# The first chunk's sums over the taps move from VectorE to TensorE, and the low products go to the end of their sums

## The chip, the cores and the metric

The kernel runs on one core of one Trainium2 chip. The metric is the device time of one execution in microseconds; the median of three runs of the kernel before is 1714.68 us (1714.65 to 1714.75).

## The reference

Two steps, all in float32. First a light convolution: for each of 33280 positions (8 sequences of 4160) and each of 8 heads, seven weights are made by a softmax, and the output is the weighted sum of the last seven rows of `x` (192 channels, 24 to a head). Then a feed-forward layer with a maximum over three products.

```python
w = np.exp(weight_gen - max over the 7 taps); w = w / (w.sum(-1) + 1e-09)
x_unf = x_pad[:, idx, :]                  # the 7 rows that end at each position
out = np.einsum('bshk,bskhg->bshg', w, x_unf)          # (33280, 192)
h = np.maximum(np.maximum(out @ w1, out @ w2), out @ w3)   # 192 -> 768
return h @ w_out                                        # 768 -> 192
```

The weights of the feed-forward layer arrive as float64.

## The kernel before

The 33280 positions lie as 128 partitions of 260 rows each. A chunk is 4 rows per partition, 512 positions; there are 65 chunks. The first chunk is a "super" of its own, after it three chunks share one load of `x` (tile xt) and of the tap weights (wt).

For a chunk the work goes like this. GpSimd multiplies `x` with the tap weights, one of the four rows at a time, into r (128 partitions, 192 channels by 7 taps; three buffers; L246, `product`). VectorE sums r over the taps into acc (L261, `total`). The sum is turned round: for the first three chunks by TensorE, with `nc.tensor.transpose` against the identity into two PSUM banks (L276 for channels 0 to 127, L277 for the other 64; `transpose`), for later chunks by VectorE and ScalarE. Then it is split into a high and a low float32r part, so that products of rounded parts give a float32 result: xa_hi and xa_lo for the first 128 channels, xb and xc for the rest (`parts`: L300 and L306, L308 on ScalarE, L304 and L309 on VectorE for the first three chunks).

The feed-forward weights are split likewise, and this happens once, in the opening. A piece goes through these steps in `split`: ScalarE's absolute value (L467) into a PSUM bank, three VectorE operations (L469, L471, L476), ScalarE's copy into the high part (L481), three more on VectorE that overwrite the bank or fill e (L483, L488, L492), ScalarE's f (L494), and GpSimd's product f times e into the low part (L495). The pieces have names in the program: a0 to a8 are the first 128 channels (wa_hi, wa_lo; 256 columns each), b0 to b2 the other 64 (wb_hi, wb_lo; 384 columns each, with four extra ScalarE copies, L550), d0 to d5 the last matrix (wo).

TensorE's main loop has for each chunk nine steps `up`, each two sums of 512 columns: per sum products wa_hi with xa_hi, wa_hi with xa_lo, wa_lo with xa_hi, wb_hi with xb, and in part wb_lo with xc (all at L329). The 128 rows are worked as two halves of 64 that run side by side. ScalarE copies the first of three sums to m (L376), VectorE takes the maximum with the other two (L378), ScalarE and GpSimd split the result into h_hi and h_lo (L381, L385). Four `down` tasks then multiply the chunk before with wo. The PSUM pool "ph" has eight banks, for transposes, weight pieces and sums alike.

The order of all that stands around TensorE's loop is written by hand. Time is counted in ticks, 22 to a chunk. `OPENING` maps a tick to a list of stages: `a0` carries piece a0 one step on, `s0` a softmax, `x0.1` is the product of chunk 0, row 1, `+0.1` its sum, `t0` one row's turn, `p0` a step of the split. Tick -1 holds what comes before the loop. A stage whose forerunner isn't done does that first (`stage` calls `finish`). What `OPENING` doesn't name goes by the rule tables: `ticks` places `+c.t` at 22 times (c minus a chunk count) plus a tick, from `SUMS`. Every engine keeps the order in which the instructions were written (`pin`).

Of the kernel before, what the change touches and what calls it, by code (L numbers as in the profile page):

```python
# [20 lines left out]
P = 128  # L21
# [3 lines left out]

OPENING = {
    -1: (
        "x0.0 s0 x0.1 a0 s0 a0 a0 x0.2 a0 a2 t0 +0.0 a2 b0 +0.1 a1 b0 b0 a1 +0.3 s1 a3 b0 a1 "
        "a2 s1 a1 +0.2 t0 b1 s1 x0.3"
    ),  # L30
    0: "a6 a4 a2 a3 a6",
    1: "a6 a3 b0 t0 t0",
    2: "b1 a6 s0",
    3: "a4 a5 a3",
    4: "b1 a5",
    6: "b2 +1.0 a5 x1.1 x1.0",
    7: "x1.2 s1 a4",
    8: "+1.1",
    9: "a5 b2 x1.3",
    10: "b2 b2 b1 p0",  # L40
    11: "s0 t1 +1.2",
    12: "a4 +1.3",
    14: "b1 p0",
    16: "a7 a7 a8 p1",
    17: "a7 t1",
    18: "s2 d1 d1 a8 p1",
    19: "p1 b2 a8 d2 t1",
    20: "d2 p0 d1",
    21: "d0",
    22: "d0",  # L50
    24: "a7 +2.0 d0",
    25: "d2 +2.1 d1",
    26: "d3 t1",
    27: "d0 x2.1 d3 d5 d2",
    28: "d3 x2.2",
    29: "x2.3 d3 a8 d4",
    30: "d4 x2.0",
    31: "d5",
    32: "+2.2 d4 d5",
    33: "t2 +2.3 t2 t2",  # L60
    34: "s2",
    35: "x3.0 x3.2 p2",
    36: "d4",
    38: "d5 p2 p2",
    42: "x3.1",
    43: "t3 t3",
    46: "+3.3 +3.2 +3.1 +3.0 t2",
    48: "t3",
    49: "s2",
    52: "x4.1",  # L70
    54: "t3",
    56: "x4.0 p3",
    57: "x3.3",
    58: "p3 t3 s2",
    59: "t3",
    61: "+4.1",
    66: "x4.2",
    67: "x4.3",
    68: "t3",
    69: "p3",  # L80
    74: "+4.3 +4.2",
    77: "+4.0",
}


# [7 lines left out]
LOAD = (5, 5)  # L93

ON_TENSOR = 3


@with_exitstack
def lightconv_maxout_kernel(
# [25 lines left out]
    nc = tc.nc  # L125
    B, S, D = x.shape
    H, K = weight_gen.shape[2:]
# [48 lines left out]
    state = {}  # L176

    def pin(ins):

        tc.keep_in_program_order(ins)  # L180
        return ins
# [52 lines left out]
    def product(c, t):  # L234

        s = super_of[c]
        a, n = chunks[c]
        la = a - chunks[supers[s][0]][0]
        xt, wt = state["x", s], state["w", s]
        if t == 0:  # L240
            state["acc", c] = att.tile([P, TC, D], F32, name="acc")

        r = att.tile([P, D, K], F32, name="r", bufs=3)
        state["r", c, t] = r
        pin(
            nc.gpsimd.tensor_tensor(  # L246
                r.rearrange("p (h g) k -> p k h g", g=G),
                xt[:, la + t : la + t + K].rearrange("p k (h g) -> p k h g", g=G),
                wt[:, la + t]
                .rearrange("p (h k) -> p k h", k=K)  # L250
                .unsqueeze(3)
                .broadcast_to([P, K, H, G]),
                op=ALU.mult,
            )
        )

    def total(c, t):

        r = state.pop(("r", c, t))
        pin(  # L260
            nc.vector.tensor_reduce(  # L261
                state["acc", c][:, t], r, axis=AX.X, op=ALU.add
            )
        )

    def transpose(c):


        acc = state["acc", c]
        if c < ON_TENSOR:  # L270
            pa, pb = (ps.tile([P, CH], F32, name="ph") for _ in range(2))
            pb = pb[:DB]
            state["p", c] = pa, pb
            for t in range(TC):
                to = slice(t * P, (t + 1) * P)
                pin(nc.tensor.transpose(pa[:, to], acc[:, t, :P], ident))  # L276
                pin(nc.tensor.transpose(pb[:, to], acc[:, t, P:], ident))  # L277
                yield
            return
        v = xtp.tile([P, NJ * D * 2], F32, name="room", bufs=1)  # L280
        pa, pb = v[:, :CH], v[DB:, CH : 2 * CH]
        state["p", c] = pa, pb
        blocks = v[:, 2 * CH : 2 * CH + TC * D].rearrange("p (t d) -> p t d", t=TC)
        pin(nc.vector.transpose(blocks, acc))  # L284
        yield
        for f in range(0, D, 32):
            to = pa[f : f + 32] if f < P else pb[f - P : f - P + 32]
            to = to.rearrange("f (t p) -> f t p", t=TC)
            for p in range(0, P, 32):
                pin(nc.scalar.copy(to[:, :, p : p + 32], blocks[p : p + 32, :, f : f + 32]))  # L290
            yield

    def parts(c):
# [8 lines left out]

        eng, at = (nc.vector, halves[0]) if c < ON_TENSOR else (nc.gpsimd, halves[1])
        pin(eng.tensor_tensor(xa_lo, pa, xa_hi.bitcast(F32), op=ALU.subtract))  # L304
# [20 lines left out]
    def product_of(ph, terms, half, key, begins=True, ends=True):  # L325

        h = halves[half]
        for q, (n, w, v) in enumerate(terms):
            ins = nc.tensor.matmul(  # L329
                ph[:, :n],  # L330
                w[h],
                v[h],
                start=begins and half == 0 and q == 0,
                stop=ends and half == 1 and q == len(terms) - 1,
            )
# [242 lines left out]
    def stage(name):  # L578
# [19 lines left out]
    def finish(name):  # L598
        while stage(name) != "done":
            pass  # L600
# [32 lines left out]
    for c in range(NC + 1):  # L633
        for tick in range(TICKS):
# [10 lines left out]
            k, odd = divmod(tick - (TC if tick >= 2 * DOWN_AT else 0), 2)  # L645
# [5 lines left out]
            if c == NC:  # L651
# [4 lines left out]
                elif tick >= 2 * DOWN_AT + TC and tick < 2 * DOWN_AT + 2 * TC:  # L656
                    t = tick - 2 * DOWN_AT - TC
# [44 lines left out]
```

## Time and profile before

| | |
|---|---|
| median of three runs | 1714.68 us |
| the profiled execution | 1714.73 us |
| its span, first to last instruction | 1712.9 us |
| TensorE busy, matmuls | 1668.9 us, 97% |
| GpSimd busy | 1427.9 us, 83% |
| ScalarE busy | 1138.6 us, 66% |
| VectorE busy | 1135.5 us, 66% |
| L261, the sums over the taps | 260 of them, 401.9 us, mean 1547 ns |
| L276 and L277, transposes on TensorE | 12 of each |

Rows of a timeline show the start in microseconds, the length, the engine, the line, the operation with output and inputs, and in brackets how long the engine stood idle before and what ended that. Lengths of neighbours on one engine overlap a little, so the distance from start to start is what an instruction costs in a queue. The chain rows show a start, a length and whose work it is. The view by stretches gives for each engine the busy microseconds and the instructions in that stretch.

### The profile page before, as it was taken

The page shows a single profiled execution, that of the slowest core. Times are in us where ns is not written, and L with a number is a line of the kernel's source. Part 1 is how long each engine was busy: PE and PEld are TensorE (multiplying, and loading weights), DVE is VectorE, ACT ScalarE, POOL GpSimd, SP SyncE. Part 2 cuts the span into 40 slices and gives each one's busy share as a digit, 9 for nine tenths or more (in the row PEclk, how much of TensorE's full clock was granted, in tenths as well). Part 3 has the DMA queues.
Part 4 walks back from the last instruction along what each step waited for, and adds up shares of the span by engine and source line. Part 5 has one row for each costly group of instructions (what it writes and reads, how often), then busy time and mean ns, then how long its engine had stood idle before and what let it go on. Part 6 is the DMA issues. An engine that isn't in the chain of part 4 may idle for free.

```text
span 1712.9 us, 42123 instructions
## 1 busy us (share of the span) xinstructions
PE 1668.9 (97%) x16794; PEld 1639.7 (96%) x16794; DVE 1135.5 (66%) x1570; ACT 1138.6 (66%) x2878; POOL 1427.9 (83%) x844
## 2 busy tenths in 40 slices
PE   3799999999999999999999999999999999999999
PEld 2589999999999999999999999999999999999999
DVE  7967666666666666766666666666666666666653
ACT  3556667667667667666766766766766766676672
POOL 5888888989888888888888898988889888888872
PEclk9999999999999999999999999999999999999999
DMA  7010101101010110101010110101011010101000
GB/s 234 1 69 11 69 20 60 69 20 60 20 70 10 70 43 38 69 20 67 13 70 20 60 69 20 60 20 69 11 69 49 31 69 20 69 11 46 20 11 29
DMA packets 20422, 79.50 MB, mean 46 GB/s; under 512 B 2321, under 2 KB 5129, under 8 KB 17537
## 3 DMA queue, kind: packets, MB, share of 16 engines
q1 hardware_dynamic: 20104, 76.54, 11.8%
q8 instruction: 131, 2.15, 0.5%
q14 instruction: 67, 0.54, 0.1%
q10 hardware_dynamic: 120, 0.28, 0.1%
HBM read 51.25 MB, written 25.56 MB: 45 GB/s over the span
## 4 chain that ended last, share of the span: by engine, by line
PE 94%; DVE 4%; DMA 1%; issue 0%; SPq 0%; ACT 0%; DVEq 0%; ACTq 0%
PE ph L329 94%; DVE acc L261 1%; DVE m L378 1%; DVE ph L471 0%; DVE e L492 0%; DVE ph L476 0%; DMA h_lo<-in_moe_w_dram 0%; DVE ph L488 0%; DVE ph L469 0%; DVE ph L483 0%; DMA xt<-in_x_dram 0%; SPq L526 0%; DVE red L215 0%; SPq L518 0%; DVE xb L309 0%
## 5 line engine op out<-in xcount | busy, mean ns | idle before, releaser
L246 POOL TENSOR_TENSOR r<-xt,wt 128x1344 f32<-128x1344 f32 x260 | 721.8, 2817 | 0.7 <-DMA xt<-in_x_dram 0.4
L378 DVE TENSOR_TENSOR m<-ph,m 128x512 f32<-128x512 f32 x780 | 522.8, 685 | 215.4 <-PE ph L329 115.8
L385 POOL TENSOR_TENSOR h_lo<-m,h_hi 128x512 fp32r<-128x512 f32 x390 | 503.3, 1302 | 169.3 <-ACT h_hi L381 164.5
L329 PE MATMUL ph<-xa_hi,wa_hi 64*128 64x512 f32 x2340 | 627.5, 390 | 5.6 <-ACT f L494 3.4
L329 PE MATMUL ph<-xa_lo,wa_hi 64*128 64x512 f32 x2340 | 624.8, 388 | 2.5 <-DVE xa_lo L304 2.5
L329 PE MATMUL ph<-xa_hi,wa_lo 64*128 64x512 f32 x2340 | 624.3, 388 | 2.8 <-POOL wa_lo L495 2.7
L329 PE MATMUL ph<-xb,wb_hi 64*128 64x512 f32 x2340 | 623.9, 387 | 0.0
L329 PE MATMUL ph<-wo,h_hi 64*128 64x384 f32 x3120 | 596.1, 358 | 0.0
L329 PE MATMUL ph<-wo,h_lo 64*128 64x192 f32 x3120 | 554.9, 249 | 0.0
L381 ACT CAST h_hi<-m 128x512 fp32r<-128x512 f32 x390 | 242.0, 621 | 403.9 <-DVE m L378 400.9
L329 PEld LDWEIGHTS ph<-wo,h_hi 64*128 64x128 f32 x3120 | 486.3, 184 | 7.3 <-POOL wo L495 0.2
L329 PEld LDWEIGHTS ph<-wo,h_lo 64*128 64x128 f32 x3120 | 484.8, 187 | 0.1
L261 DVE TENSOR_REDUCE acc<-r 128x192 f32<-128x1344 f32 x260 | 401.9, 1547 | 109.7 <-POOL r L246 109.7
L290 ACT COPY room<-room 32x128 f32<-32x128 f32 x1488 | 440.6, 296 | 26.7 <-DVE room L284 8.5
L329 PE MATMUL ph<-xc,wb_lo 64*128 64x512 f32 x1170 | 453.3, 387 | 1.4 <-POOL wb_lo L495 1.4
L329 PEld LDWEIGHTS ph<-xa_hi,wa_hi 64*128 64x128 f32 x2340 | 364.3, 185 | 12.7 <-ACT f L494 4.2
L329 PEld LDWEIGHTS ph<-xa_hi,wa_lo 64*128 64x128 f32 x2340 | 357.6, 185 | 6.8 <-POOL wa_lo L495 4.4
L329 PEld LDWEIGHTS ph<-xa_lo,wa_hi 64*128 64x128 f32 x2340 | 357.6, 185 | 5.1 <-DVE xa_lo L304 3.0
L329 PEld LDWEIGHTS ph<-xb,wb_hi 64*128 64x128 f32 x2340 | 357.8, 185 | 2.5
L376 ACT COPY m<-ph 128x512 f32<-128x512 f32 x390 | 222.0, 586 | 57.1 <-PE ph L329 49.6
L411 DVE TENSOR_TENSOR o<-ph,ob 128x192 f32<-128x192 f32 x260 | 86.5, 353 | 237.5 <-ACT ob L410 237.5
L329 PEld LDWEIGHTS ph<-xc,wb_lo 64*128 64x128 f32 x1170 | 216.0, 185 | 3.6 <-POOL wb_lo L495 1.8
(57 smaller groups left out, 699.7 us busy)
## 6 DMA issues: line engine op xcount, KB each, us to landing
xt<-in_x_dram SPq DMA_DIRECT2D x20, 1728.0 KB, 6.8
out_dram<-o SPq DMA_DIRECT2D x64, 384.0 KB, 2.3
wt<-in_weight_gen_dram SPq DMA_DIRECT2D x21, 336.0 KB, 3.0
h_hi<-in_moe_w_dram SPq DMA_DIRECT2D x6, 256.0 KB, 5.5
xt<-in_x_dram SPq DMA_DIRECT2D x1, 1536.0 KB, 9.3
h_lo<-in_moe_w_dram SPq DMA_DIRECT2D x6, 192.0 KB, 5.6
room<-in_moe_w_out_dram SPq DMA_DIRECT2D x1, 1152.0 KB, 7.6
xt<-in_x_dram SPq DMA_DIRECT2D x1, 960.0 KB, 5.1
```

The lines of the kernel that those rows point to most:

```text
L246: nc.gpsimd.tensor_tensor(r.rearrange("p (h g) k -> p k h g", g=G), xt[:, la + t : la + t + K].rearrange("p k (h g) -> p k h g", g=G), wt[ ...
L261: nc.vector.tensor_reduce(state["acc", c][:, t], r, axis=AX.X, op=ALU.add)
L290: pin(nc.scalar.copy(to[:, :, p : p + 32], blocks[p : p + 32, :, f : f + 32]))
L329: ins = nc.tensor.matmul(ph[:, :n], w[h], v[h], start=begins and half == 0 and q == 0, stop=ends and half == 1 and q == len(terms) - 1,)
L376: pin(nc.scalar.copy(m[:, :N], ph[:, :N]))
L378: pin(nc.vector.tensor_tensor(m[:, :N], ph[:, :N], m[:, :N], op=ALU.max))
L381: later(1, lambda: pin(nc.scalar.copy(hi, m[:, :N])))
L385: nc.gpsimd.tensor_tensor(lo, m[:, :N], hi.bitcast(F32), op=ALU.subtract)
L411: pin(nc.vector.tensor_tensor(o[:, t], po[:, :D], ob, op=ALU.add))
```

## The change

Three edits.

For chunk 0 (`SUMS_ON_TENSOR`), VectorE's four sums are left out (`total` returns at once, no acc is made). In `transpose` TensorE multiplies the seven taps of r, each a slice with a step of seven elements, by the identity into one PSUM region, so that the seven products add up there: 2 x 7 products for each of four rows, 56 in all, in float32, where 8 transposes were. r stays in use until its products are done.

In `up` the product of wa_lo and xa_hi goes from the third place of a sum to the last.

The table `OPENING` is another one. It no longer names the sums `+0.0` to `+0.3`, so the rule puts them at ticks below -1; they do nothing themselves, but each first finishes its product, so that the four products of chunk 0 are written ahead of everything else of tick -1.

```diff
 OPENING = {
     -1: (
-        "x0.0 s0 x0.1 a0 s0 a0 a0 x0.2 a0 a2 t0 +0.0 a2 b0 +0.1 a1 b0 b0 a1 +0.3 s1 a3 b0 a1 "
-        "a2 s1 a1 +0.2 t0 b1 s1 x0.3"
+        "a0 a0 a1 a0 a0 a1 a1 x0.1 x0.3 x0.0 t0 t0 a2 x0.2 s0 a2 b0 b0 b0 s1 a3 b1 b0 a2 s1 "
+        "a1 b1 s0 a3 s1 t0 t0 a6"
     ),
-    0: "a6 a4 a2 a3 a6",
-    1: "a6 a3 b0 t0 t0",
+    0: "a6",
+    1: "a6 a3 a4 b0 a6",
...
+SUMS_ON_TENSOR = (0,)
...
-        if t == 0:
+        if t == 0 and c not in SUMS_ON_TENSOR:
             state["acc", c] = att.tile([P, TC, D], F32, name="acc")
...
     def total(c, t):
 
+        if c in SUMS_ON_TENSOR:
+            return
         r = state.pop(("r", c, t))
...
             for t in range(TC):
                 to = slice(t * P, (t + 1) * P)
-                pin(nc.tensor.transpose(pa[:, to], acc[:, t, :P], ident))
-                pin(nc.tensor.transpose(pb[:, to], acc[:, t, P:], ident))
+                if c in SUMS_ON_TENSOR:
+                    r = state.pop(("r", c, t))
+                    for k in range(K):
+                        for ph, f in ((pa, slice(0, P)), (pb, slice(P, D))):
+                            pin(
+                                nc.tensor.matmul(
+                                    ph[:, to], r[:, f, k], ident, start=k == 0, stop=k == K - 1
+                                )
+                            )
+                else:
+                    pin(nc.tensor.transpose(pa[:, to], acc[:, t, :P], ident))
+                    pin(nc.tensor.transpose(pb[:, to], acc[:, t, P:], ident))
                 yield
...
-            terms = [(wa_hi[:, j, i], xa_hi), (wa_hi[:, j, i], xa_lo), (wa_lo[:, j, i], xa_hi)]
-            terms.append((wb_hi[:, j, i], xb))
+            terms = [(wa_hi[:, j, i], xa_hi), (wa_hi[:, j, i], xa_lo), (wb_hi[:, j, i], xb)]
             if half == odd:
                 terms.append((wb_lo[:, jp, i], xc))
+            terms.append((wa_lo[:, j, i], xa_hi))
```

VectorE, in the opening, from the first half of a2 on (bank ph_183; ph_164 is a1, wt_115 the next super's tap weights). Before:

```order
L476 SCALAR_TENSOR_TENSOR ph_183<-h_hi_85,ph_183 128x256
L261 TENSOR_REDUCE acc_144<-r_197 128x192
L215 TENSOR_REDUCE red_200<-wt_115 128x96
L483 TENSOR_SCALAR ph_183<-h_hi_85 128x256
L488 SCALAR_TENSOR_TENSOR ph_183<-h_hi_85,ph_183 128x256
L492 TENSOR_SCALAR e_184<-ph_183 128x256
L483 TENSOR_SCALAR ph_164<-h_hi_85 128x256
L488 SCALAR_TENSOR_TENSOR ph_164<-h_hi_85,ph_164 128x256
L492 TENSOR_SCALAR e_165<-ph_164 128x256
L261 TENSOR_REDUCE acc_144<-r_160 128x192
L224 TENSOR_REDUCE den_201<-wt_115 128x96
```

And the same place now, from the end of b0 on (ph_206 is a2, ph_235 the first half of b1, ph_230 a3):

```order
L508 TENSOR_SCALAR e_216<-ph_214 128x384
L219 TENSOR_REDUCE red_226<-wt_115 128x96
L499 TENSOR_SCALAR ph_206<-h_hi_85 128x256
L504 SCALAR_TENSOR_TENSOR ph_206<-h_hi_85,ph_206 128x256
L508 TENSOR_SCALAR e_207<-ph_206 128x256
L485 TENSOR_SCALAR ph_235<-ph_235 128x384
L487 TENSOR_SCALAR ph_235<-ph_235 128x384
L492 SCALAR_TENSOR_TENSOR ph_235<-h_lo_86,ph_235 128x384
L485 TENSOR_SCALAR ph_230<-ph_230 128x256
```

No sum stands between the pieces any more; a1's second half has gone ahead of b0, and b1's first half comes before den.

GpSimd, the products of chunk 0 and what follows them (r_145 to r_197 before, with f_151 and e_150 of piece a0):

```order
L246 TENSOR_TENSOR r_160<-xt_89,wt_90 128x7x192
L495 TENSOR_TENSOR wa_lo_81<-f_151,e_150 128x2x128 [waits Activation_49]
L246 TENSOR_TENSOR r_197<-xt_89,wt_90 128x7x192 [waits DVE_49]
L217 TENSOR_TENSOR wt_115<-wt_115,red_200 128x672 [waits DMAHW6_49,DVE_49]
L495 TENSOR_TENSOR wb_lo_83<-f_180,e_179 128x384 [waits Activation_49]
```

Now (r_144 to r_150; f_154 and e_153 of a0):

```order
L250 TENSOR_TENSOR r_148<-xt_89,wt_90 128x7x192
L250 TENSOR_TENSOR r_150<-xt_89,wt_90 128x7x192 [waits PE_49,Pool_49]
L511 TENSOR_TENSOR wa_lo_81<-f_154,e_153 128x2x128 [waits Activation_49]
L221 TENSOR_TENSOR wt_115<-wt_115,red_226 128x672 [waits DMAHW6_49,DVE_49]
L511 TENSOR_TENSOR wb_lo_83<-f_217,e_216 128x384 [waits Activation_49]
```

The fourth product now waits for TensorE in the place of VectorE, and a0's low part stands behind it.

TensorE, from the last row's turn of chunk 0 into the first sums (ph_169, ph_170 the two banks of the turn). Before:

```order
L276 MATMUL ph_169<-ident_79,acc_144 128x128
L277 MATMUL ph_170<-ident_79,acc_144 64x128
L329 MATMUL ph_271<-xa_hi_261,wa_hi_80 128x512
L329 MATMUL ph_271<-xa_lo_262,wa_hi_80 128x512
L329 MATMUL ph_271<-xa_hi_261,wa_lo_81 128x512
L329 MATMUL ph_271<-xb_263,wb_hi_82 128x512
L329 MATMUL ph_271<-xc_264,wb_lo_83 128x512
```

And now:

```order
L287 MATMUL ph_176<-ident_79,r_150 128x128
L287 MATMUL ph_177<-ident_79,r_150 64x128
L345 MATMUL ph_311<-xa_hi_301,wa_hi_80 128x512
L345 MATMUL ph_311<-xa_lo_302,wa_hi_80 128x512
L345 MATMUL ph_311<-xb_303,wb_hi_82 128x512
L345 MATMUL ph_311<-xc_304,wb_lo_83 128x512
L345 MATMUL ph_311<-xa_hi_301,wa_lo_81 128x512
```

The pair of L287 stands seven times for each row, and the product with wa_lo has moved to the end of the sum.

More of the change, by code (lines that the diff above doesn't have):

```diff
@@ L27 @@
     -1: (
-        "x0.0 s0 x0.1 a0 s0 a0 a0 x0.2 a0 a2 t0 +0.0 a2 b0 +0.1 a1 b0 b0 a1 +0.3 s1 a3 b0 a1 "
-        "a2 s1 a1 +0.2 t0 b1 s1 x0.3"
-    ),
-    0: "a6 a4 a2 a3 a6",
-    1: "a6 a3 b0 t0 t0",
-    2: "b1 a6 s0",
-    3: "a4 a5 a3",
+        "a0 a0 a1 a0 a0 a1 a1 x0.1 x0.3 x0.0 t0 t0 a2 x0.2 s0 a2 b0 b0 b0 s1 a3 b1 b0 a2 s1 "
+        "a1 b1 s0 a3 s1 t0 t0 a6"
+    ),
+    0: "a6",
+    1: "a6 a3 a4 b0 a6",
+    2: "a5",
+    3: "a2 a4 s0 a3",
     4: "b1 a5",
-    6: "b2 +1.0 a5 x1.1 x1.0",
-    7: "x1.2 s1 a4",
+    5: "s1",
+    6: "+1.0 x1.1 x1.0 a5 b2",
+    7: "x1.2 a4",
     8: "+1.1",
[L39 to L49, printed above, removed]
+    9: "a5 x1.3",
+    10: "b1 b2 b1 b2 b2",
+    11: "t1 p0 +1.2",
+    12: "a7 a4 s0 t1",
+    14: "+1.3",
+    16: "a7 a8 p1",
+    17: "a7",
+    18: "s2 d1 a8 p1",
+    19: "d2 d1 a8",
+    20: "b2 t1 p0 d2 d0 p0 d1",
+    21: "p1 d0",
     22: "d0",
-    24: "a7 +2.0 d0",
+    24: "a7 +2.0",
     25: "d2 +2.1 d1",
[L53 to L58, printed above, removed]
+    26: "x2.1",
+    27: "d0 d5 d2",
+    28: "x2.3 a8 d4 x2.0",
+    29: "d3",
+    30: "x2.2 d4 d3",
+    31: "d3 t1 d5",
     32: "+2.2 d4 d5",
-    33: "t2 +2.3 t2 t2",
+    33: "t2 +2.3 t2 t2 d3",
     34: "s2",
[L62 to L68, printed above, removed]
+    35: "x3.0 x3.2",
+    36: "p2 d4",
+    37: "d5",
+    38: "p2 p2",
+    42: "x3.1 t3",
+    44: "+3.1 t3",
+    46: "+3.3 +3.2 x3.3 +3.0",
+    47: "t3",
     49: "s2",
-    52: "x4.1",
+    53: "x4.1 t3",
     54: "t3",
[L72 to L79, printed above, removed]
+    57: "x4.0 t3 p3",
+    58: "p3",
+    60: "s2",
+    61: "x4.3 +4.1",
+    64: "t3",
+    67: "x4.2",
+    68: "t2",
     69: "p3",
-    74: "+4.3 +4.2",
+    74: "+4.2",
     77: "+4.0",
+    80: "+4.3",
 }
@@ L266, in transpose @@
     def transpose(c):
-        acc = state["acc", c]
+        acc = state.get(("acc", c))
         if c < ON_TENSOR:
```

## The prediction

> **What bounds the kernel now.** I read the page's busy line and its chain first, then the chain in order of time, then the stretches of ten microseconds, and last the timelines of VectorE, ScalarE, TensorE and GpSimd in the opening.
>
> ```profile
> PE 1668.9 (97%) x16794; PEld 1639.7 (96%) x16794; DVE 1135.5 (66%) x1570; ACT 1138.6 (66%) x2878; POOL 1427.9 (83%) x844
> PE 94%; DVE 4%; DMA 1%; issue 0%; SPq 0%; ACT 0%; DVEq 0%; ACTq 0%
> ```
> ```profile
> 86.00 3.30 PE ph L329 x27
> 89.67 7.44 PE ph L329 x87
> 105.44 70.37 PE ph L329 x587
> ```
> ```profile
> core 0: us, PE busy (x) PEld busy (x) DVE busy (x) ACT busy (x) POOL busy (x), PEclk, DMA share, GB/s
> 30.00:40.00 10.00, 7.46 (x28) 5.48 (x29) 9.38 (x22) 4.11 (x10) 3.71 (x4) 1.00 0.67 259
> 40.00:50.00 10.00, 6.17 (x44) 4.10 (x43) 9.79 (x18) 5.35 (x12) 9.12 (x6) 1.00 0.00 0
> 80.00:90.00 10.00, 8.71 (x73) 6.15 (x71) 9.72 (x20) 4.96 (x12) 9.02 (x8) 1.00 0.00 0
> 90.00:100.00 10.00, 10.00 (x122) 9.63 (x120) 6.32 (x11) 5.33 (x12) 9.91 (x6) 1.00 0.01 2
> ```
>
> TensorE is the chain for 94% of the span, but not in the opening: from 86 us on the chain is TensorE, and before that TensorE is busy only 6 to 9 us in ten while VectorE is busy 9.4 to 9.8. So the program is an opening of about 86 us that VectorE sets, with the splitting of the weights, the sums over the taps and the maxima in one queue, and then 1627 us in which TensorE streams. The change alters the amount of work of that long part by nothing: the same products stand in it, with two of them in another order. What the change is worth is how much earlier the opening hands over.
>
> **VectorE's queue before.** The rows that I add up from (start, length, idle before where there is any):
>
> ```profile
> 9.10 0.43 DVE L469 TENSOR_SCALAR ph<-ph 128x256 f32<-128x256 f32 x1 [2.33 <-ACT ph L467]
> 12.17 1.54 DVE L261 TENSOR_REDUCE acc<-r 128x192 f32<-128x1344 f32 x1
> 14.89 1.54 DVE L261 TENSOR_REDUCE acc<-r 128x192 f32<-128x1344 f32 x1
> 17.44 0.57 DVE L469 TENSOR_SCALAR ph<-ph 128x384 f32<-128x384 f32 x1 [1.00 <-ACT ph L467]
> 20.64 0.42 DVE L469 TENSOR_SCALAR ph<-ph 128x256 f32<-128x256 f32 x1
> 21.90 1.54 DVE L261 TENSOR_REDUCE acc<-r 128x192 f32<-128x1344 f32 x1
> 23.36 0.84 DVE L215 TENSOR_REDUCE red<-wt 128x96 f32<-128x672 f32 x1
> 24.12 0.42 DVE L483 TENSOR_SCALAR ph<-h_hi 128x256 uint32<-128x256 uint32 x1
> 26.64 1.54 DVE L261 TENSOR_REDUCE acc<-r 128x192 f32<-128x1344 f32 x1
> 28.09 0.84 DVE L224 TENSOR_REDUCE den<-wt 128x96 f32<-128x672 f32 x1
> 29.89 0.41 DVE L469 TENSOR_SCALAR ph<-ph 128x256 f32<-128x256 f32 x1
> 32.40 0.68 DVE L304 TENSOR_TENSOR xa_lo<-ph,xa_hi 128x512 fp32r<-128x512 f32 x1
> 33.72 0.41 DVE L483 TENSOR_SCALAR ph<-raw_a 128x256 uint32<-128x256 uint32 x1
> 36.36 0.56 DVE L469 TENSOR_SCALAR ph<-ph 128x384 f32<-128x384 f32 x1
> 38.03 0.43 DVE L469 TENSOR_SCALAR ph<-ph 128x256 f32<-128x256 f32 x1
> 42.08 0.68 DVE L378 TENSOR_TENSOR m<-ph,m 128x512 f32<-128x512 f32 x1
> ```
>
> **What is removed.** Four sums (L261) leave VectorE. In the queue one takes 21.90 to 23.36, 1.46 us, so 5.84 us in all. If nothing else stopped VectorE, that would be the gain; so I walk the new queue past the waits that the sums used to cover.
>
> Up to 17.44 the two first sums go, and the queue has three pieces of weight there instead of one and a half: six operations of a0, six of a1, the first three of a2, each 0.46 apart. From 9.10 that is 6.9 us and two short waits of 0.44 for ScalarE's copy of the high part, so 16.9. The next piece, b0, can't come sooner than its data, which ScalarE's first step takes up at 16.89 in the rows below; it starts at 17.44 as before. The 2.92 us of those two sums thus buy only a1's second half, three operations, which cost 1.26 later (24.12 to 26.64 holds two such halves).
>
> ```profile
> 16.89 0.52 ACT L467 ACTIVATE ph<-h_lo 128x384 f32<-128x384 f32 x1 [3.92 <-DMA h_lo<-in_moe_w_dram]
> 20.30 0.49 ACT L494 ACTIVATE f<-ph 128x384 f32<-128x384 uint32 x1 [0.28 <-DVE ph L488]
> 20.68 2.06 ACT L550 CAST wb_hi<-hi 64x384 fp32r<-64x384 f32 x4
> 22.77 0.65 ACT L481 CAST wa_hi<-ph 128x256 fp32r<-128x256 f32 x2
> 27.04 0.40 ACT L467 ACTIVATE ph<-raw_a 128x256 f32<-128x256 f32 x1
> 40.82 0.59 ACT L376 COPY m<-ph 128x512 f32<-128x512 f32 x1 [1.17 <-PE ph L329]
> ```
>
> From 17.44: b0 ends at 20.64, the maximum of the next weights (0.76, 23.36 to 24.12) at 21.40. Then comes a2's second half, which overwrites the bank that ScalarE must first copy to wa_hi. That copy stands behind the four copies of b0's high part, now also behind one more first step (b1's), which I estimate to push it by 0.15: 22.77 becomes 22.9, and VectorE goes on at 23.25. **VectorE waits here 1.85 us for ScalarE**; before, the third sum filled this place. After that: a2's half 1.26 (24.5), b1's first three 36.36 to 38.03 = 1.67 (26.2), a3's first three 1.25 (27.4), den and its reciprocal 28.09 to 29.89 = 1.80 (29.2), a6's first three 1.25 (30.5; its data is there at 27.04), xa_lo and xb 32.40 to 33.72 = 1.32 (31.8), the halves of a6 and a3 33.72 to 36.36 = 2.64 (34.5), and a4, b1's rest and a5 38.03 to 42.08 = 4.05 (38.5). There the first maximum that VectorE does for TensorE stands, at 42.08 before, with the same work done ahead of it in both programs. VectorE is 3.6 us early: 5.84 less the 1.85 and less some 0.4 of small waits.
>
> **What is added to TensorE.** Fifty-six products with the identity in the place of eight transposes, all before the first weight product.
>
> ```profile
> 28.71 0.42 PE L276 MATMUL ph<-ident,acc 128*128 128x128 f32 x1
> 28.93 0.42 PE L277 MATMUL ph<-ident,acc 128*64 128x128 f32 x1
> 33.13 0.79 PE L329 MATMUL ph<-xa_lo,wa_hi 64*128 64x512 f32 x1 [2.54 <-DVE xa_lo L304]
> 34.15 0.62 PE L329 MATMUL ph<-xb,wb_hi 64*128 64x512 f32 x1
> 34.58 0.62 PE L329 MATMUL ph<-xc,wb_lo 64*128 64x512 f32 x1
> 40.99 0.39 PE L329 MATMUL ph<-xa_hi,wa_hi 64*128 64x512 f32 x1
> 41.22 0.39 PE L329 MATMUL ph<-xa_lo,wa_hi 64*128 64x512 f32 x1
> ```
> ```profile
> 7.86 7.65 POOL L246 TENSOR_TENSOR r<-xt,wt 128x1344 f32<-128x1344 f32 x3 [0.37 <-DMA xt<-in_x_dram]
> ```
>
> The trace of before holds no plain float32 product. The nearest row by shape is the transpose, 0.22 from start to start (28.71 to 28.93); that is the lower bound. A row that streams four times the columns through the same array has 0.43 (34.15 to 34.58) while TensorE is slow, and 0.23 (40.99 to 41.22) later. An upper bound is four transposes for one product, 0.88 slow and 0.44 later, if float32 needs four passes each with its own weight load. I take 0.43 and 0.22, since a pass that loads while it streams is what the weight products show. The granted clock reads 1.00 in both stretches, so I go by the spacing, which halves some 7 us after 33.13.
>
> The Trainium skill, TensorE: Matmul & The Clock Gate, section Terms, says that the transpose mode is four times faster for float32. By that sentence a product here would be an estimated 0.88 and 0.44; no row of before shows one.
>
> The first product tile comes off GpSimd at 7.86 + 2.55 = 10.4. Its fourteen products end at 10.4 + 6.0 = 16.4, and only then is the buffer free for GpSimd's fourth tile (three buffers): 16.4 to 19.0, and behind it in GpSimd's queue the low part of a0. Waiting for that low part is VectorE's e of a2, which it reaches at 24.2; it holds up to 24.2 with ease. With 7 us slow, TensorE has done 16 of 56 by 17.4, and the rest at 0.22 ends at 26.2. ScalarE's xa_hi follows at 27.4 (it has a6's first step at 27.04 ahead of it), and xa_lo is wanted only at 30.5. So the 56 products are **hidden behind VectorE**, with 4 us to spare. Slow to the end they would take 24 us, end at 34.5, and cost about 4.7 of the 3.6.
>
> **What TensorE gives back.** With xa_lo at 30.5, its first product with it starts at 31.2, 1.9 earlier than at 33.13. Its third sum was ready not before 41.7: ScalarE copied the second at 40.82, and four more products take 0.9. That is 8.6 after 33.13, so now 39.8. VectorE, there at 38.5, waits 1.3, and the 3.6 become 2.3. If the clock rises sooner, less is lost; the bounds of this term are 1.9 and 3.6.
>
> **The other edits.** That wa_lo comes last in a sum lets a product wait for GpSimd two or three places later. TensorE isn't the bound before 86 us, so this is worth 0 there, and nothing after it, where no product waits for wa_lo; it could give up to 0.4. The table's other moves leave the number of VectorE's operations as it is. VectorE's idle is 0.21 in the stretch from 40 and 0.28 in that from 80; five such stretches from 40 to 90 are an estimated 1.4 in all. I take 0 for these moves, between a gain of 1.4 and a loss of the same.
>
> **Sum:** 1714.73 (the profiled execution: span 1712.9 and 1.8 around it) less 2.3 is 1712.4; the median of the runs is 0.05 lower, so **1712.3 us**.
>
> **The rivals.**
>
> *The whole gain, or most of it.* VectorE isn't held by TensorE at the maximum and the idle later on goes: 3.6 + 1.4 = 5.0, or at most the full 5.84, so 1708.9 to 1711.2. For it: TensorE has been at work since 10.4 and may reach its fast spacing sooner. Against it: a gap of some 5 us between the last identity product and 31.2. Chance 0.33.
>
> *The dear product.* One product costs four transposes: 8 of them in 7 slow us, then 48 at 0.44 are 21.1, so the last ends at 10.4 + 28.1 = 38.5 and xa_lo comes at 39.3 in the place of 30.5. VectorE stands 8.8 us in front of xa_lo with all of the splitting behind it, 3.6 - 8.8 = -5.2, 1719.9 us. It decides from about 0.34 a product on, at the later spacing. For it: a transpose takes 0.22 for 128 columns, half and not a quarter of the 0.43 for 512, so something beside the columns is paid in it. Against it: the weight products hide their loads. The page's sentence above is this rival. Chance 0.15, with any other late xa_lo.
>
> *It moves nothing.* VectorE's wait for ScalarE's copies and its wait for TensorE take up nearly all, and the end shifts by less than 1.2: 1713.5 to 1715.9. The two waits are in my sum already, at 3.2 of 5.84; this needs another one. Chance 0.14.
>
> **Numbers.** The forecast, a gain between 1.2 and 3.4, has 0.38. A measurement here tells 0.2%, 3.4 us, from no change, so forecast and the third rival are both "same": 0.52. Faster has 0.33 and slower 0.15. The range reaches from 1709.2, most of the first rival, to 1717.0, into the second; the likeliest case alone has 1711.3 to 1713.5.
>
> **What would show it.** In the changed profile: VectorE has no L261 row before 40; at about 21.4 it waits near 1.9 us for ScalarE's wa_hi copy; xa_lo stands at about 30.5; the first maximum at about 39.8 with a wait for TensorE; the 56 products lie 0.43 and then 0.22 apart and end near 26; the chain turns to TensorE for good near 83.7. Wrong would be: xa_lo held by ScalarE's xa_hi, a product spacing above 0.34 late in the row, or a GpSimd that stands long in front of its fourth tile.

## The result and the profile after

The changed kernel takes 1734.68 us, the median of four runs (1733.94 to 1735.01), against 1714.66 us for the kernel before (1714.53 to 1714.75, four runs). The ratio is 1.0116, with an interval of 1.01 to 1.0132: slower by 20 us, on the other side of no change than forecast, and outside the range.

The page of the changed kernel, its busy line and its chain by engine:

```profile
PE 1706.5 (98%) x16898; PEld 1666.2 (96%) x16898; DVE 1130.8 (65%) x1566; ACT 1138.4 (66%) x2878; POOL 1428.5 (82%) x844
PE 95%; DVE 3%; POOL 1%; ACT 1%; issue 0%; DMA 0%; SPq 0%; DVEq 0%; POOLq 0%; ACTq 0%
```

TensorE is busy 37.6 us longer than before, and it has 104 matmul records more. By the code there are 48 more, 56 products in the place of 8 transposes. If each of the 56 leaves two records, 112 less 8 make the 104. That is the first sign of what a float32 product is here. The timeline of TensorE in the changed kernel shows the products as one group, and what follows them:

```profile
10.84 38.90 PE L287 MATMUL ph<-ident,r 128*128 128x128 f32 x112 [10.84 <-POOL r L250]
49.78 0.79 PE L345 MATMUL ph<-xa_hi,wa_hi 64*128 64x512 f32 x1
52.24 0.62 PE L345 MATMUL ph<-xc,wb_lo 64*128 64x512 f32 x1
52.67 0.62 PE L345 MATMUL ph<-xa_hi,wa_lo 64*128 64x512 f32 x1
...
59.70 0.39 PE L345 MATMUL ph<-xa_hi,wa_lo 64*128 64x512 f32 x1
59.93 0.39 PE L345 MATMUL ph<-xc,wb_lo 64*128 64x512 f32 x1
```

The 56 products take 38.90 us without a pause, 0.69 each, and end at 49.7; the forecast had 26.2. Behind them the weight products still stand 0.43 apart (52.24 to 52.67) and reach 0.23 (59.70 to 59.93) only at about 59. The column of the granted clock reads 1.00 in all this time, so the spacing is what tells here. So 38.9 us of unbroken work had not brought TensorE to its later spacing. Its weight loads in the changed kernel show the two records:

```profile
13.61 0.53 PEld L287 LDWEIGHTS ph<-ident,r 128*128 128x128 f32 x2 [0.32 <-issue]
14.37 0.31 PEld L287 LDWEIGHTS ph<-ident,r 128*64 128x64 f32 x2 [0.22 <-issue]
15.00 0.54 PEld L287 LDWEIGHTS ph<-ident,r 128*128 128x128 f32 x2 [0.32 <-issue]
```

Each product has two loads. From 13.61 to 15.00 a pair (128 channels, then 64) costs 1.39 us: 0.76 for the first and 0.63 for the second.

VectorE's queue in the changed kernel, at the places that the prediction named, and what GpSimd and ScalarE waited for:

```profile
23.88 0.43 DVE L499 TENSOR_SCALAR ph<-h_hi 128x256 uint32<-128x256 uint32 x1 [1.76 <-ACT wa_hi L497]
30.85 0.43 DVE L492 SCALAR_TENSOR_TENSOR ph<-raw_a,ph 128x256 uint32<-128x256 uint32 x1
49.76 0.69 DVE L320 TENSOR_TENSOR xa_lo<-ph,xa_hi 128x512 fp32r<-128x512 f32 x1 [18.48 <-ACT xa_hi L316]
59.90 0.69 DVE L394 TENSOR_TENSOR m<-ph,m 128x512 f32<-128x512 f32 x1 [0.26 <-PE ph L345]
```
```profile
20.76 2.64 POOL L250 TENSOR_TENSOR r<-xt,wt 128x1344 f32<-128x1344 f32 x1 [4.92 <-PE ph L287]
49.15 0.58 ACT L316 CAST xa_hi<-ph 128x512 fp32r<-128x512 f32 x1 [21.45 <-PE ph L287]
53.81 2.11 POOL L511 TENSOR_TENSOR wa_lo<-f,e 128x256 fp32r<-128x256 f32 x3 [26.60 <-ACT f L510]
```

VectorE is done with its work ahead of xa_lo at 31.3 (30.85 and 0.43) and then stands 18.48 us, for ScalarE's xa_hi, which itself stood 21.45 us for the products of TensorE. All of the splitting behind xa_lo stands with it, GpSimd's low parts among it (26.60 us). The stretches of the changed kernel (columns as in the prediction) show who works and who doesn't:

```profile
30.00:40.00 10.00, 10.00 (x31) 5.94 (x29) 1.21 (x4) 0.00 (x0) 0.00 (x0) 1.00 0.74 289
40.00:50.00 10.00, 9.95 (x30) 6.08 (x29) 0.24 (x1) 0.81 (x2) 0.00 (x0) 1.00 0.00 0
```

Before, VectorE was busy 9.38 and 9.79 here; now it is 1.21 and 0.24, with TensorE full. The bound of the opening has changed engine. The first maximum for TensorE stands at 59.90 instead of 42.08, 17.8 late, of a total of 20.0.

### The profile page after: what moved, and what is told of

It reads as the page before. It is cut to its first block, busy times and chain, and to the rows that moved or that the text cites. A ratio compares the mean times of both kernels' runs of the same rounds, so it can differ in the third digit from the quotient of the medians.

```text
span 1732.7 us, 42398 instructions
## 1 busy us (share of the span) xinstructions
PE 1706.5 (98%) x16898; PEld 1666.2 (96%) x16898; DVE 1130.8 (65%) x1566; ACT 1138.4 (66%) x2878; POOL 1428.5 (82%) x844
## 4 chain that ended last, share of the span: by engine, by line
PE 95%; DVE 3%; POOL 1%; ACT 1%; issue 0%; DMA 0%; SPq 0%; DVEq 0%; POOLq 0%; ACTq 0%
PE ph L345 92%; PE ph L287 2%; POOL r L250 1%; DVE acc L267 1%; DVE m L394 1%; DMA xt<-in_x_dram 0%; DVE ph L487 0%; DVE ph L492 0%; ACT room L306 0%; DVE ph L504 0%; DVE e L508 0%; DVE ph L499 0%; DVE ph L485 0%; ACT m L392 0%; POOL h_lo L401 0%
## 5 line engine op out<-in xcount | busy, mean ns | idle before, releaser
L267 DVE TENSOR_REDUCE acc<-r 128x192 f32<-128x1344 f32 x256 | 395.7, 1547 | 110.0 <-POOL r L250 110.0
```

The costliest lines, as they stand in the source:

```text
L267: nc.vector.tensor_reduce(state["acc", c][:, t], r, axis=AX.X, op=ALU.add)
```

## The experiments

Three theories were to be told apart. By the **price** theory the whole loss is the price of the product with the identity, 0.69 us 56 times, and xa_lo behind it. By the **table** theory the new order of the opening costs by itself. By the **clock** theory the products are dear only since TensorE is slow when they come. For the price there was then the question why a product is that dear.

**One tap of seven on TensorE** (`one_tap`). The changed kernel with only the first tap of chunk 0 multiplied by the identity, 8 products as there were 8 transposes before; the other six taps of the first 512 positions are left out of the sum.

```diff
-                    for k in range(K):
+                    for k in range(1):
...
-                                    ph[:, to], r[:, f, k], ident, start=k == 0, stop=k == K - 1
+                                    ph[:, to], r[:, f, k], ident, start=True, stop=True
```

> The changed kernel with one tap of seven for chunk 0: 8 products with the identity in the place of 56, so that chunk 0's output holds one tap alone. All else as changed. Theory 'price' (the 56 products alone make it slower; 38.9 us in the trace of the changed kernel, 0.69 us each): 8 products take 5.6 us and end with the fourth tile off GpSimd near 20 us, xa_lo stands at about 31.2 where VectorE reaches it, and the time is that of the prediction's sum, 1712.4 us (1711.0 to 1713.5). Rival 'table' (the new order of the opening or of the sums costs by itself): 1716 us or more, with xa_lo early all the same.

Measured: 1714.49 us, ratio 1.0000 (0.999 to 1.0009). Nearly the whole loss is gone with the 48 products. The timeline of this kernel at the two places of the prediction:

```profile
30.73 0.68 DVE L320 TENSOR_TENSOR xa_lo<-ph,xa_hi 128x512 fp32r<-128x512 f32 x1
38.07 0.56 DVE L508 TENSOR_SCALAR e<-ph 128x384 uint32<-128x384 uint32 x1 [0.95 <-ACT hi L497]
40.01 0.69 DVE L394 TENSOR_TENSOR m<-ph,m 128x512 f32<-128x512 f32 x1
```

xa_lo and the first maximum are where the prediction had put them, 30.5 and 39.8. Between this kernel and the changed one the first maximum moves by 59.90 - 40.01 = 19.9 us, and 1714.5 + 19.9 = 1734.4, against 1734.68 measured. That carries the loss. What was missed is smaller: the first maximum is 2.1 earlier than before, and yet the time isn't 1712.4 but 1714.5, above the expected range. The chain of this kernel shows TensorE taking over behind the opening at 104.87, where it was 105.44 before:

```profile
101.67 1.56 DVE acc L267
...
104.16 0.66 DVE m L394
104.82 0.04 issue
104.87 30.26 PE ph L345 x252
```

So 1.5 us are given back between 40 and 105 us. The later part of the table is where the two kernels differ there; `old_tail` below takes that up.

**Low product last, alone** (`lo_last`). The kernel before with the product of wa_lo moved to the end of a sum, and nothing else.

```diff
-            terms = [(wa_hi[:, j, i], xa_hi), (wa_hi[:, j, i], xa_lo), (wa_lo[:, j, i], xa_hi)]
-            terms.append((wb_hi[:, j, i], xb))
+            terms = [(wa_hi[:, j, i], xa_hi), (wa_hi[:, j, i], xa_lo), (wb_hi[:, j, i], xb)]
...
+            terms.append((wa_lo[:, j, i], xa_hi))
```

> The kernel before with one edit: the product of wa_lo and xa_hi last in a sum; the opening's table and the sums on VectorE as before. Theory: TensorE is not the bound in the opening and waits for no low part after it, so 1714.2 to 1714.8 us, no change. Rival (the order of the products matters to TensorE's stream): a shift of more than 3.4 us either way.

Measured: 1714.83 us, ratio 0.9999 (0.999 to 1.0008). This edit is worth nothing, as forecast.

**The taps laid out one behind the other** (`contig`). In the change the loaded operand is a slice of r with a step of seven elements. Here r of chunk 0 is laid out tap by tap, so that each slice is contiguous for TensorE.

```diff
         r = att.tile([P, D, K], F32, name="r", bufs=3)
+        if c in SUMS_ON_TENSOR:
+            r = r.rearrange("p d k -> p (d k)").rearrange("p (k d) -> p d k", k=K)
```

> The changed kernel, with the product tile of chunk 0 laid out tap by tap, so that the slice TensorE loads for a product has its 128 columns side by side and not 28 bytes apart. Same products, same result. Theory 'passes' (a float32 product is two records, whatever the layout): still 0.69 us for a product, 38.9 us for 56, 1734.7 us. Theory 'stride' (the spread columns make the load slow): the record pair falls towards the transposes' 0.22 to 0.45 us, the 56 end between 23 and 36 us, and the time falls to 1713 to 1722 us.

Measured: 1732.71 us, ratio 1.0105 (1.0085 to 1.0125). TensorE's timeline in this kernel:

```profile
10.30 37.78 PE L289 MATMUL ph<-ident,r 128*128 128x128 f32 x112 [10.30 <-POOL r L252]
```

37.78 for 56 is 0.675 a product, 0.02 less than with the step. The products begin 0.5 earlier and take 1.1 less, which is most of the 2.0 us that this kernel is faster than the changed one. The layout isn't the cause of the other 18.

**A warm TensorE** (`warm`). The changed kernel with 24 idle bf16 products of 512 columns ahead of everything, so that TensorE comes to the first product at its later spacing. The work added is thrown away.

```diff
+    warm = const.tile([P, CH], mybir.dt.bfloat16, name="warm")
+    pin(nc.gpsimd.memset(warm, 1.0))
+    pw = ps.tile([P, CH], F32, name="ph")
+    for _ in range(24):
+        pin(nc.tensor.matmul(pw, warm[:, :P], warm, start=True, stop=True))
```

> The changed kernel with 24 idle bfloat16 products of 512 columns on TensorE from about 2 us on, ahead of the first product with the identity; they write a bank that nobody reads. Theory 'slow array' (the products cost 0.69 us since the array stands at half speed and they don't raise it themselves): the first ones after the idle products cost 0.35 us; if they hold the speed, all end near 31 us and the time is 1711 to 1714 us; if they lose it after some microseconds, they end between 40 and 47 us and the time is 1724 to 1732 us. Theory 'load' (the weight load sets the price, whatever the array's speed): 0.69 us each, 1733 to 1737 us.

Measured: 1733.18 us, ratio 1.0108 (1.0087 to 1.0128). The products still take 38 us. TensorE's timeline in this kernel, then its loads, then the stretches:

```profile
1.83 7.40 PE L584 MATMUL ph<-warm 128*128 128x512 bf16 x24 [1.83 <-POOL warm L581]
10.63 38.29 PE L287 MATMUL ph<-ident,r 128*128 128x128 f32 x112 [1.41 <-POOL r L250]
```
```profile
10.63 0.30 PEld L287 LDWEIGHTS ph<-ident,r 128*128 128x128 f32 x1 [1.90 <-POOL r L250]
11.72 0.30 PEld L287 LDWEIGHTS ph<-ident,r 128*128 128x128 f32 x1
12.80 0.30 PEld L287 LDWEIGHTS ph<-ident,r 128*128 128x128 f32 x1
```
```profile
12.00:13.00 1.00, 1.00 (x5) 0.76 (x5) 0.93 (x4) 0.38 (x1) 1.00 (x1) 0.92 1.12 257
13.00:14.00 1.00, 1.00 (x4) 0.64 (x4) 0.76 (x2) 0.17 (x1) 1.00 (x2) 0.50 1.14 237
20.00:30.00 10.00, 10.00 (x30) 6.17 (x30) 7.85 (x17) 5.05 (x12) 6.21 (x5) 0.50 0.70 225
```

For the first two microseconds a pair of products takes 1.09 (10.63 to 11.72 to 12.80), 0.54 a product; that is between the 0.35 and the 0.69 of the two theories. Then the granted clock, 0.92 between 12 and 13, is 0.50 from 13 on, with TensorE busy all the time, and the price is the old one. Two things follow. The clock that was there is lost some 2 us into the products and doesn't come back while they run; that the 1.41 us for which TensorE stood ahead of them had a part in the loss isn't excluded. And even at 0.54 all the way 56 of them would be 30 us and end near 41, later than the 30 us at which VectorE wants them. The clock theory explains only a part of the price, and work ahead of the products didn't bring that part.

**Float32r in the place of float32** (`f32r`). The products of chunk 0 take r and the identity as float32r; the sums of the first 512 positions then go through this rounded type.

```diff
+        if c in SUMS_ON_TENSOR:
+            r = r.bitcast(F32R)
...
-                                    ph[:, to], r[:, f, k], ident, start=k == 0, stop=k == K - 1
+                                    ph[:, to], r[:, f, k], ident_r, start=k == 0, stop=k == K - 1
...
+    ident_r = const.tile([P, P], F32R, name="ident_r")
+    pin(nc.scalar.copy(ident_r, ident))
```

> The changed kernel with chunk 0's product tile and the identity in the rounded float32r type in place of float32, all 56 products kept; chunk 0's output is of lower precision. Theory 'passes' (a float32 product is two loads and two runs through the array, a float32r product one): one record for a product, 0.22 to 0.43 us each, the last between 23 and 35 us; below 0.36 they hide behind VectorE and the time is that of one tap alone, 1714.5 us (1713.5 to 1716). Rival 'late start of the sums for another reason' (the fourth tile on GpSimd, the tap slices' layout): 0.6 us or more each and 1725 us or more.

Measured: 1713.74 us, ratio 0.9995 (0.9986 to 1.0004). The profile is of an execution of 1716.04 us, 2.3 above the median. The timeline of TensorE in this kernel, and then the loads for 128 channels up to 52 us, as a group, in the changed kernel and in this one (behind the bars the busy time, the mean of one in ns, and the idle time before them):

```profile
11.29 10.41 PE L289 MATMUL ph<-ident_r,r 128*128 128x128 f32 x56 [11.29 <-POOL r L252]
```
```profile
L287 PEld LDWEIGHTS ph<-ident,r 128*128 128x128 f32 x56 | 15.0, 315 | 19.5 <-POOL r L250 10.8 <-issue 8.6
L289 PEld LDWEIGHTS ph<-ident_r,r 128*128 128x128 f32 x28 | 9.1, 325 | 11.4 <-POOL r L252 11.3
```

One record a product in the place of two: 28 loads for 128 channels where the changed kernel has 56. The same 56 products take 10.41 us, 0.19 each, and xa_lo stands at 30.74, as with one tap. So it is the float32 form of the product that costs. One part of it is the second record: 38.90 us for 112 records is 0.35 a record. The other part is that a float32 record takes 0.35 where a float32r record takes 0.19. Its load isn't longer, 315 ns against 325; but between the loads of the changed kernel TensorE's load side stands idle for nothing that the profile shows (8.6 us before these 56), and in this kernel the loads follow each other without that. Why the float32 records stand apart like this no run here shows.

**Four taps** (`four_taps`). As `one_tap`, with 4 of the 7 taps, so 32 products; three taps of the first 512 positions are left out.

```diff
-                    for k in range(K):
+                    for k in range(4):
...
-                                    ph[:, to], r[:, f, k], ident, start=k == 0, stop=k == K - 1
+                                    ph[:, to], r[:, f, k], ident, start=k == 0, stop=k == 3
```

> The changed kernel with four taps of seven for chunk 0: 32 products; chunk 0's output holds four taps. Theory 'price': 10.7 + 32 x 0.69 = 32.9 us for the last, xa_lo near 33.5 in the place of 30.7, 2.8 us above the 1714.5 us of one tap: 1717.3 us (1716 to 1719). Rival 'any delay of TensorE is swallowed up to 8 us' (its work in the opening has slack): 1714.5 us.

Measured: 1717.55 us, ratio 1.0016 (1.0007 to 1.0025). TensorE and VectorE in the timeline of this kernel:

```profile
11.20 22.26 PE L287 MATMUL ph<-ident,r 128*128 128x128 f32 x64 [11.20 <-POOL r L250]
33.49 0.69 DVE L320 TENSOR_TENSOR xa_lo<-ph,xa_hi 128x512 fp32r<-128x512 f32 x1 [3.21 <-ACT xa_hi L316]
```

The price per product is the same, 22.26 / 32 = 0.70, and the stop is 3.21 us in the place of 18.48. With 8 products nothing, with 32 three us, with 56 twenty: the loss begins where TensorE ends after about 30 us, and from there it is TensorE's time one for one (the 24 products more take 38.90 - 22.26 = 16.6 us, and the two medians are 17.1 apart).

**The old later part of the table** (`old_tail`). `one_tap` with the rows of `OPENING` from tick 9 on as the kernel before has them (of these rows the first differ like this):

```diff
-    9: "a5 x1.3",
-    10: "b1 b2 b1 b2 b2",
-    11: "t1 p0 +1.2",
-    12: "a7 a4 s0 t1",
-    14: "+1.3",
+    9: "a5 b2 x1.3",
+    10: "b2 b2 b1 p0",
+    11: "s0 t1 +1.2",
+    12: "a4 +1.3",
+    14: "b1 p0",
...
```

> One tap for chunk 0, with the opening's table as changed up to tick 8 and as it was before from tick 9 on. In the run of one tap the first maximum came 2.07 us early (40.01 for 42.08), but TensorE's last step of the chain only 0.6 us (104.87 for 105.44). Theory 'tail' (the new table's later part gives up what the earlier part won): the lead stays, 1712.5 to 1713.3 us. Rival 'not the table' (TensorE at half speed after its gaps, whatever the table): 1714 to 1715 us.

Measured: 1712.23 us, ratio 0.9986 (0.9977 to 0.9995), against 1714.49 for `one_tap`; it is a little below the expected range. Here are the stretches from 80 to 90 of `one_tap`, then those from 70 to 90 of this kernel, and then the chain of this kernel:

```profile
80.00:85.00 5.00, 3.36 (x18) 1.93 (x20) 4.72 (x12) 3.20 (x8) 4.62 (x4) 0.82 0.00 0
85.00:90.00 5.00, 5.00 (x52) 4.58 (x49) 4.57 (x7) 1.11 (x3) 4.31 (x4) 0.84 0.00 2
```
```profile
70.00:75.00 5.00, 3.17 (x20) 2.03 (x18) 4.79 (x11) 2.57 (x7) 4.29 (x7) 0.85 0.01 3
75.00:80.00 5.00, 5.00 (x39) 4.26 (x36) 4.79 (x12) 1.71 (x5) 5.00 (x2) 0.81 0.00 0
80.00:85.00 5.00, 4.54 (x40) 3.44 (x38) 4.79 (x11) 3.18 (x8) 3.96 (x6) 1.00 0.00 0
85.00:90.00 5.00, 5.00 (x61) 4.41 (x60) 4.09 (x7) 2.86 (x6) 5.00 (x3) 1.00 0.01 3
```
```profile
86.47 14.73 PE ph L341 x151
102.31 12.77 PE ph L341 x105
```

From the first maximum (38.88 here) to TensorE's take-over (102.31) it is 63.4 us, as before the change (42.08 to 105.44, 63.4); with the new later part it is 64.9 in `one_tap` and in the changed kernel alike (59.90 to 124.79). In these profiles the new later part thus costs some 1.5 us. The rest of the 2.3 between the medians can't be put down to it: in its profile xa_lo already stands 0.9 earlier (29.80 instead of 30.73), since ScalarE's first step of b0, which waits for a DMA, starts at 16.14 instead of 17.09; up to there the order is the same.

The place of the 1.5 us can be seen in VectorE's timeline, first of `one_tap`, then of this kernel. The row is VectorE's first addition for a `down` task, which waits for ScalarE's copy ob of TensorE's result:

```profile
92.06 0.36 DVE L427 TENSOR_TENSOR o<-ph,ob 128x192 f32<-128x192 f32 x1 [2.42 <-ACT ob L426]
89.18 0.36 DVE L423 TENSOR_TENSOR o<-ph,ob 128x192 f32<-128x192 f32 x1 [0.91 <-ACT ob L422]
```

The wait is 2.2 to 2.5 us in all seven kernels with the new later part and 0.9 in the five with the old one, the kernel before and `lo_last` among them. Just ahead of it, at the four maxima that begin at 87.16 in `one_tap`, the lag behind the old later part is only 0.2 us. In front of the wait, 42 to 50 us after its own first maximum, the granted clock is 0.79 in six of the seven kernels and 0.57 in `f32r`; in the five it is 1.00. A lower clock by itself isn't the loss, though: this kernel has it ten microseconds sooner (0.85 and 0.81 from 70 to 80), and its four maxima at 85.80 stand 46.9 us after the first as they do before the change. That TensorE, after a stop of 1.57 us for ScalarE's copy of m at 83 us in `one_tap`, runs slower just where VectorE needs its next result is argued from these twelve profiles. No run takes away that stop or that clock alone.

**Two rows of four** (`two_rows`). A version with the full result: rows 0 and 1 of chunk 0 are summed on TensorE, 28 products; rows 2 and 3 stay on VectorE and are put in the queue after the tap weights' maximum (row 2) and ahead of den (row 3).

```diff
-    -1: (
-        "a0 a0 a1 a0 a0 a1 a1 x0.1 x0.3 x0.0 t0 t0 a2 x0.2 s0 a2 b0 b0 b0 s1 a3 b1 b0 a2 s1 "
-        "a1 b1 s0 a3 s1 t0 t0 a6"
-    ),
+    -1: 'x0.2 a0 a0 a1 a0 a0 a1 a1 t0 t0 a2 x0.3 s0 a2 b0 b0 b0 s1 +0.2 a3 b1 b0 a2 s1 a1 b1 s0 a3 +0.3 s1 t0 t0 a6',
...
-SUMS_ON_TENSOR = (0,)
+ROWS_ON_TENSOR = ((0, 0), (0, 1))
...
-        if c in SUMS_ON_TENSOR:
+        if (c, t) in ROWS_ON_TENSOR:
...
```

> The changed kernel with two of chunk 0's four rows summed on TensorE (28 products) and two on VectorE as before, one of these where VectorE waited 1.8 us for ScalarE; the full result. Theory 'price': the 28 end at 10.7 + 19.4 = 30.1 us, the last transposes near 31, xa_lo near 32.5 us where it stood at 32.4 before, with b1's first half done ahead: 1714 to 1715.5 us, no longer slower than before and 19 to 20.5 us below the changed kernel. Rival 'products on TensorE slow the opening whatever their number': 1720 us or more.

Measured: 1716.05 us, ratio 1.0007 (0.9998 to 1.0016), 0.6 above the expected range. The timelines of TensorE and VectorE in this kernel:

```profile
10.79 19.48 PE L284 MATMUL ph<-ident,r 128*128 128x128 f32 x56 [10.79 <-POOL r L247]
32.44 0.68 DVE L317 TENSOR_TENSOR xa_lo<-ph,xa_hi 128x512 fp32r<-128x512 f32 x1
```

28 products of 0.70 end at 30.3 and hold nobody up. That the gain is so small comes from VectorE's queue, which the rest of its timeline in this kernel shows:

```profile
17.89 0.57 DVE L482 TENSOR_SCALAR ph<-ph 128x384 f32<-128x384 f32 x1 [1.35 <-ACT ph L480]
21.85 1.54 DVE L264 TENSOR_REDUCE acc<-r 128x192 f32<-128x1344 f32 x1
23.68 0.43 DVE L496 TENSOR_SCALAR ph<-h_hi 128x256 uint32<-128x256 uint32 x1 [0.29 <-ACT wa_hi L494]
27.94 1.54 DVE L264 TENSOR_REDUCE acc<-r 128x192 f32<-128x1344 f32 x1
41.37 0.68 DVE L391 TENSOR_TENSOR m<-ph,m 128x512 f32<-128x512 f32 x1
```

The sum at 21.85 is free: VectorE waits 0.29 for ScalarE's copy behind it, where it waited 1.76 in the changed kernel without that sum. The one at 27.94 costs its full 1.47 (27.94 to 29.41). The two that left VectorE stood ahead of b0, where VectorE waits for data in any case, 1.35 here. So the first maximum is only 0.7 earlier than before (42.08), and the new later part of the table takes that back and more.

**Two combinations.** `two_rows_old_tail` is `two_rows`, and `f32r_old_tail` is `f32r`, each with the later part of the table as the kernel before has it, the same edit as in `old_tail`. The first has the full result; in the second the sums of the first 512 positions go through the rounded type, as in `f32r`.

> Two rows of chunk 0 on TensorE in float32, two on VectorE, and the table of before from tick 9 on; the full result. Theory (they add): the 1716.0 us of the two rows less the 2.3 us that the later part gave back with one tap, 1713.8 us (1713 to 1714.7). Rival (the later part of the table costs only where the opening is early): 1715.5 to 1717 us.

> All 56 products of chunk 0 in the rounded float32r type (lower precision in chunk 0), and the table of before from tick 9 on. Theory (the price of a float32 product and the new table's later part are the two things that cost, and they add): as one tap with the old later part, 1712.2 us (1711.5 to 1713.3), some 2.4 us below the kernel before. Rival (the 56 products still cost something in the opening, or the two don't add): 1713.7 to 1715 us.

Measured: 1715.10 us, ratio 1.0002 (0.9993 to 1.0011), for the two rows, 0.4 above the expected range; and 1712.77 us, ratio 0.9988 (0.9979 to 0.9997), for float32r. Both are faster with the old later part, by 0.95 and 0.97, less than the 2.3 that was expected of it for the two rows. In their profiles the way from the first maximum to TensorE's take-over is 63.5 and 63.6 us, against 65.1 and 66.2 with the new later part; the 66.2 is from the profile of `f32r`, with its granted clock of 0.57. So by three pairs of medians the new later part costs between 1 and 2.3 us. The executions lie further apart with it too: 1714.38 to 1717.07 for `two_rows`, 1714.58 to 1715.55 with the old later part. The float32r version beats both kernels by time, by 1.9 us against the one before, but with the rounded sums in its first chunk. No version with the full result came out faster than the kernel before.

## Why the prediction was wrong

- *VectorE bounds the opening, and a gain there is handed on to TensorE's long part.* Right. With few products on TensorE the walk of the new queue holds: the wait for ScalarE's copy to wa_hi, forecast as 1.85 us, is 1.76; VectorE is free for xa_lo at 31.3, where 30.5 was forecast; with one tap xa_lo stands at 30.73 and the first maximum at 40.01 (39.8). The prediction let TensorE set that maximum, 8.6 us after its first product with xa_lo, and it came 8.5 after (31.47); but VectorE was hardly ahead of it, for of the 1.3 us that it was to stand there 0.95 went to a wait for ScalarE at 38.07 that the walk didn't have. From the take-over to the end the profiles of all twelve kernels here need 1607.5 to 1608.2 us, whether it comes at 102 or at 125. But the take-over isn't at 86 us, as the prediction had it: the chain of the kernel before goes through four of VectorE's sums once more from 97.84 on, and TensorE has it for good from 105.44.
- *What is added to TensorE.* **This is the step that failed.** The prediction took 0.43 a product while TensorE is slow and 0.22 after some 7 us of work. The product costs 0.69, the later spacing doesn't come in 38.9 us of work, and the 56 end at 49.7, not at 26.2. Two choices were wrong in it. "A pass that loads while it streams" was taken from products with 512 columns, one record each, 0.43 apart; here a product is two records, 0.35 each. And the rise of the clock was taken from those same weight products, while these products didn't bring it about, and it was lost under them (`warm`). The upper bound, 0.88 and 0.44, was stated and was wide enough for the price at the start, but not for the price later on.
- *The cover.* The 56 products were to be hidden behind VectorE, with a break-even at 0.34 for the products after the first 16, which is 0.37 over all 56. That point was about right: in the changed kernel the products may take 38.90 - 18.48 = 20.4 us before VectorE stands, 0.36 each, and with four taps 22.26 - 3.21 = 19.05, 0.34 each. The measured 0.69 is twice that, and even the 0.54 of a warm TensorE is above it.
- *The rival of the dear product* named the mechanism and the place: xa_lo late, VectorE in front of it with all of the splitting behind. It said 1719.9 since it too let the price fall to half after 7 us. The sentence of the Trainium skill (TensorE: Matmul & The Clock Gate, section Terms) that stood beside it, that the transpose mode is four times faster for float32, agrees in direction: 0.69 against 0.22 for a transpose is 3.1 times, both at the slow spacing; with TensorE at its later spacing it is 0.54 (`warm`) against 0.11 (55.94 to 56.05 in the kernel before), 4.9 times. What no row of before could show was the missing rise.
- *The order of the products in a sum* was taken at 0 and is 0 (`lo_last`, 0.9999).
- *The table's other moves* were taken at 0, between a gain and a loss of 1.4. They are a loss of 1 to 2.3 us by the medians, 1.5 by the profiles of `one_tap` and `old_tail`, at the far end of that range or beyond it: what is left of the 2.3 us in `one_tap` is nothing that can be measured. The loss falls behind 86 us, in the part that the prediction took for TensorE's alone. With the old later part 1712.23 us come out, near the 1712.3 of the forecast; that is partly luck, since 0.9 of it is b0's earlier start. So the forecast would have missed by 1.4 to 2.2 us even if the products had been hidden (`f32r`, `one_tap`). That the times of `one_tap` and of `lo_last` are the same as before isn't the same kind of zero: in the first a gain and a loss cancel.
- *GpSimd's fourth product* was to wait for TensorE until 16.4; it waits 4.92 us, until 20.76, by the same price. It decided nothing, since VectorE stood longer.

Still open are by which of its moves the new later part loses its 1 to 2 us, and why the two records of a float32 product stand 0.35 apart; no run here splits either.

## What to carry to other kernels

Before work goes to an engine that looks idle, multiply its count by a price that was measured for that form of instruction (here a float32 product of 128 columns is two records and 0.69 us, three transposes' worth), and set the result beside the time until the next engine wants it. Don't count on such work to bring the clock up; look for the spacing of the instructions after it. When a change also carries a rewritten order of work, run the order by itself: here a loss of 20 us hid another of 1 to 2 that was not of the same cause.

## What the runs showed of the hardware

- A float32 product with 128 columns leaves two records and two loads, 0.69 us; the same as float32r leaves one record, 0.19 us, though a load for 128 channels is as long (325 against 315 ns); a transpose of the same shape took 0.22.
- Unbroken float32 products of this kind didn't bring the clock up in 38.9 us. After bf16 products the granted clock was 0.92 between 12 and 13 us and 0.50 after that (`warm`), and it stayed there until the products ended. TensorE had stood 1.41 us ahead of them and had no pause within them.
- The price follows the granted clock only in part: it was 0.54 just before that fall and is 0.69 at a granted clock of 0.50, so a good part of it doesn't scale with it.
- A step of 28 bytes between the loaded elements costs 0.02 us a product (`contig`).
- The column of the granted clock can read 1.00 where the spacing says half: it does so in the changed kernel between 30 and 50 us, with 0.69 a product and 0.43 for 512 columns right behind, and reads 0.50 in `warm` at nearly the same spacing.
